# First MLP, last eight tiles: the back product as seven half-size products in place of the plain sum over sixteen steps

## The chip, the cores and the metric

The kernel runs on one core of a Trainium2 chip. The metric is the device time of one execution in microseconds (us), the median of three runs. Lower is better.

## What is computed

The reference, cut to its arithmetic. Shapes: 4 x 8 heads, 576 positions, head size 64, chunks of 64; so 2304 tokens of 512 features, 18 tiles of 128 tokens.

```python
scores = scale * np.matmul(q_c, k_c.transpose(0, 1, 2, 4, 3))     # per chunk of 64
attn = np.exp(scores - np.max(scores, axis=-1, keepdims=True))
attn = attn / (np.sum(attn, axis=-1, keepdims=True) + 1e-09)
x = np.matmul(attn, v_c)            # then heads beside each other: 2304 x 512
h = x @ w_in                        # first MLP, w_in 512 x 2048
y = (h * (1.0 / (1.0 + np.exp(-h)))) @ w_out
out = ((y @ w_a) * (y @ w_b)) @ w_out2      # second MLP, d_ff 1536
```

Weights arrive as 64-bit floats. Every product is made from operands split into a high and a low part, with three matmuls (high·high, high·low, low·high) for one.

## The kernel before, in words

The features of a token lie on the 128 partitions, so an activation tile is four column groups (`KT` = 4) of 128 x tokens. The tokens of the first MLP form five blocks: 4, 2, 4, 4 and 4 tiles (`blocks`); the block of two tiles (`SIDE`) runs beside the first one. The first MLP runs block after block, and within a block over 16 slices of d_ff (`MA` = 16). One step k is one (block, slice). `front` (`front_a`, `product`, L385) makes h for one slice, 12 matmuls of 128x512; ScalarE (ACT) applies silu twice (L413: `g` and its high part `ghi`), VectorE (DVE) takes the low part (`glo`, L411). `back` (`back_a`, L431) multiplies by w_out and adds into four PSUM banks `acc0..acc3` over the 16 slices, again 12 matmuls (4 column groups x 3). The front of step k+1 stands ahead of the back of step k in TensorE's program, so that silu and split lie beside matmuls. After the last slice the four banks are copied out and stored to DRAM (`finish_a`).

The second MLP already works on 2x2 blocks with seven products and fifteen additions (`front_product`, `back`, bank letters in `BANK`): three rounds (`PAIRS`) of 768 tokens. Its weights are needed as seven combinations, split in high and low; `comb_sums` and the splits after it make them, tiles called `ring` hold them, and DRAM buffers `wg` and `w2` keep them for later rounds.

Everything stands in a hand-written order per engine (no scheduler). In the first 16 steps (the first loop) the string `order` gives the order of the short names: `sc` = `scaled`, `mg` = `magnitude`, `bg` = `begin`, `up`/`lw` = split of a first-MLP weight, `fr` = front, `si` = its silu, `fi` = glo, `ba0`/`ba1` = halves of back, `sf`/`ss`/`sfi`/`sb` the same for the side block, S M E N T P V X L the pieces of attention for the next block (scores, maximum, exponential, normalising, transposing and copying, values and their splits). A new attention tile begins every third step.

One unit of weight conversion is a 128x512 piece of 64-bit words: a DMA into one of three raw buffers (`fetch`, SyncE's (SP's) queue), a clamp on DVE (`magnitude`, L158), two ACT operations (`scaled`, L169 and L171), and an assembly on DVE into a 32-bit tile `w` (`begin`, L181). For the second MLP `w` goes out to DRAM (`wf`). For the first MLP it is split into `wA` on ACT and DVE. Before, the first loop converts two first-MLP units a step; the 36 units of the second MLP follow, one per step, in steps 14 to 49. In the last block's steps (`in_last`) the combinations of the second MLP are made: all six of the output weight and the first of the gated ones.

Of the kernel before, what the change touches and what calls it, by code (L numbers as in the profile page):

```python
# [28 lines left out]
def chunk_attention_silu_mlp_gated_mlp(  # L29
# [50 lines left out]
    main = [b for b in range(NBLK) if b != SIDE]  # L80
    LAST = main[-1]
# [9 lines left out]
    RING = 7  # L91

# [24 lines left out]
    raws = spool.tile([P, RAWS, DM], U64, tag="raw", name="raws", bufs=1)  # L117
# [6 lines left out]
    wf = {}  # L124
    stage_1 = []
# [7 lines left out]
    def fetch(src, dest):  # L133
        raw = raws[:, turn[0] % RAWS]
        turn[0] += 1
        nc.sync.dma_start(out=raw, in_=src)
        fetched.append([dest, raw, False])
# [36 lines left out]
    def begin():  # L174
# [10 lines left out]
        if dest[0] == "f":  # L185
            wf[dest[1:]] = d = dram.tile([P, DM], F32, name=f"wf{dest[1]}{dest[2]}")
            leaving.append((d, w))
        else:
            stage_1.append((dest, w))

    def upper():
        if not stage_1:
            return
        dest, w = stage_1.pop(0)
        _, m, j = dest
        if m not in slots_a:
            slots_a[m] = slot("wA").rearrange("p (j n) -> p j n", j=4)
        hl = slots_a[m][:, 2 * j:2 * j + 2]
        nc.scalar.activation(hl[:, 0], w, AF.Copy)
        stage_2.append((dest, hl, w))  # L200
# [8 lines left out]
    def weights(src, dest):  # L209

        leave()
        fetch(src, dest)
        lower()
        scaled()
        magnitude()
        begin()
        upper()

# [11 lines left out]
    def att_tile(where, name, i=0):  # L230
        if where == "att":
# [231 lines left out]
    def comb_load(u):  # L463
        s, mat = divmod(u, 2)
        if u in (len(RING_AT) + 1, UNITS - 1):
            buf = raws[:, :2].rearrange("p a n -> p (a n)").bitcast(F32)
        else:
            buf = slot("buf", F32)
# [14 lines left out]

    def comb_split_2(s, h):
        o0, o1 = HALVES[h]
        src = bufs["o", s][:, 1 + o0:1 + o1]
        t = slot("hl").rearrange("p (o t n) -> p o t n", o=4, t=2)[:, :o1 - o0]
        nc.scalar.activation(t[:, :, 0], src, AF.Copy)
        nc.vector.tensor_tensor(
            out=t[:, :, 1], in0=src, in1=t[:, :, 0].bitcast(F32), op=ALU.subtract  # L490
        )
        w2s = w2.rearrange("p (o s) t n -> p o s t n", s=STEPS)
        nc.sync.dma_start(out=w2s[:, o0:o1, s], in_=t.bitcast(F32))
# [29 lines left out]
    kept = []  # L523
# [5 lines left out]
    def make_half():  # L529
# [3 lines left out]
        n = fed[0]  # L533
        buf = bufs[u]
# [8 lines left out]
        def lower():  # L543
# [3 lines left out]
            if n < RING:  # L547
                kept.append((wg[n], t.bitcast(F32)))
            else:
                leave()  # L550
                leaving.append((wg[n], t.bitcast(F32)))
            if h == 1 and len(RING_AT) < u + 2 < UNITS - 1:
# [11 lines left out]

    def make_now():
        make_half()
        while chores:
            chore()


# [25 lines left out]
    def refill():  # L596

        while owed[0]:
            owed[0] -= 1
            (make_half if fed[0] < 2 * UNITS else feed)()  # L600
# [6 lines left out]
    def load_pair(p, h):  # L607
        y_raw[p, h] = t = late["b"].tile([P, KT, T], F32, tag=("ca", "cb")[h], name="yr")
# [56 lines left out]
    def drain():  # L665
        leave()
        lower()
        scaled()
        magnitude()
        begin()  # L670
        upper()

# [4 lines left out]

    def prep_b():
        if done[1] < len(units_b):
            weights(*next_b())  # L680
            return True
        return False

# [10 lines left out]
    with tc.manual_schedule():  # L694
# [37 lines left out]
        def v_in(*tiles):  # L732
# [19 lines left out]
        joint = set()  # L752
# [40 lines left out]
        def plan(i, k, pos, b, o, joined, joins):  # L793
            at(k - 2, "c", lambda: load_qk(i, A))
            if joined:
                joint.add(k)
            at(k, pos, lambda: att_scores(i, (0, 1), ("at", "sB")))
# [4 lines left out]
            if joins:  # L802
                at(k + 3, "a2", lambda: att_values(i, ("at", "sB"), x_t[b], o, beside=i + 1))
# [3 lines left out]
        starts = [(2, 5, 8, 11), (18, 21, 24, 27), (33, 36, 39, 42)]  # L807
        for n, b in enumerate(main[1:]):
            at(max(starts[n][0], n * MA), "x", lambda b=b: x_t.__setitem__(b, x_tiles(width(b))))
            for t, k in enumerate(starts[n]):  # L810
                i = blocks[b][0] + t
                if n:
                    plan(i, k, "a", b, t * P, t > 0, t < 3)
                else:
                    plan_1(i, k, b, t * P)
# [3 lines left out]
        L0 = END - MA  # L819
# [95 lines left out]
        first = []  # L915

        def enter_b():
            late.pop("g")
            g_cm.__exit__(None, None, None)
            att_cm.__exit__(None, None, None)  # L920
            late["b"] = ctx.enter_context(
                tc.tile_pool(name="bpool", bufs=1, side="right", reuse_waits="tile")
            )
            for h in range(2):
                load_pair(0, h)


        def in_last(m, pos):
            if pos == "c":
                if prep_b():  # L930
                    return
                if leaving or fetched or opened or stage_1 or stage_2:
                    drain()
                if m in W2_AT:
                    comb_sums(("o", W2_AT.index(m)))
                elif m in RING_AT:
                    comb_sums(RING_AT.index(m))
                return
            if m in W2_AT:
                comb_split_2(W2_AT.index(m), int(pos == "c2"))  # L940
            if pos == "c2":
                for i in range(STEPS):
                    if W2_AT[i] == m + 2:
                        comb_load_2(i)
                for i in range(len(RING_AT)):
                    if RING_AT[i] == m + 2:
                        comb_load(i)
                if m == MA - 3:
                    comb_load(len(RING_AT))
                if m == ENTER:  # L950
                    enter_b()
            if m in RING_AT and len(ring) < RING:
                make_now()
            if m > W2_AT[-1] and kept:
                dst, src = kept.pop(0)
                nc.sync.dma_start(out=dst, in_=src)
            for f in first[:3]:
                f()
            del first[:3]

        W2_AT = [2, 3, 5, 7, 9, 11]
        RING_AT = [4, 6, 8, 10]
        ENTER = 9

        def end_last(m):
            if m == 11:
                first.extend(operands(0))

        BANKS = ("at", "sA", "sB", "mm", "acc0", "acc1", "acc2", "acc3")
        taken = [0]  # L970

        def next_bank():
            t = bank(BANKS[taken[0] % len(BANKS)], [P, T])
# [23 lines left out]
        def banks_for(o, ps):  # L997
            if o in (0, 2):
                ps[BANK[o]] = next_bank()
            return ps[BANK[o]]  # L1000

        def evacuate(o, ps, ct):
# [385 lines left out]
```

## Time and profile before

| | us |
|---|---|
| median of 3 runs (845.31 to 846.53) | 845.89 |
| the profiled execution's own time | 846.05 |
| its span, first to last instruction | 844.2 |
| TensorE (PE) busy in the span | 836.4 |
| DVE busy | 486.1 |
| ACT busy | 435.3 |
| GpSimd (POOL) busy | 54.0 |

Matmuls are pipelined, and a matmul's duration in the profile runs on into the next one; what one costs in a row is the distance between starts. The granted TensorE clock was 0.999 of full speed over the span. The execution took 1.85 us more than the span. HBM was read for 141.0 MB and written for 51.9 MB, 229 GB/s over the span.

### The profile page before, as it was taken

The page shows a single profiled execution, that of the slowest core. Times are in us where ns is not written, and L with a number is a line of the kernel's source. Part 1 is how long each engine was busy: PE and PEld are TensorE (multiplying, and loading weights), DVE is VectorE, ACT ScalarE, POOL GpSimd, SP SyncE. Part 2 cuts the span into 40 slices and gives each one's busy share as a digit, 9 for nine tenths or more (in the row PEclk, how much of TensorE's full clock was granted, in tenths as well). Part 3 has the DMA queues.
Part 4 walks back from the last instruction along what each step waited for, and adds up shares of the span by engine and source line. Part 5 has one row for each costly group of instructions (what it writes and reads, how often), then busy time and mean ns, then how long its engine had stood idle before and what let it go on. Part 6 is the DMA issues. An engine that isn't in the chain of part 4 may idle for free.

```text
span 844.2 us, 13936 instructions
## 1 busy us (share of the span) xinstructions
PE 836.4 (99%) x5442; PEld 763.5 (90%) x5442; DVE 486.1 (58%) x894; ACT 435.3 (52%) x856; POOL 54.0 (6%) x102
## 2 busy tenths in 40 slices
PE   8999999999999999999999999999999999999998
PEld 7888888888888888888889999999999999999998
DVE  5655655535444355338766997683545594454563
ACT  6956767546654566446554554462333373333252
POOL 1000000020001010023202110000000000000000
PEclk9999999999999999999999999999999999999999
DMA  8444344165555555368899788877667888666761
GB/s 300 139 161 138 131 157 147 54 231 170 174 168 175 194 185 165 121 217 319 283 381 367 305 317 321 319 279 255 259 257 274 305 304 294 244 248 245 287 236 57
DMA packets 54113, 193.85 MB, mean 230 GB/s; under 512 B 5920, under 2 KB 13728, under 8 KB 45600
## 3 DMA queue, kind: packets, MB, share of 16 engines
q1 hardware_dynamic: 46752, 169.59, 55.9%
q0 software_dynamic: 7008, 23.07, 8.3%
q8 instruction: 43, 0.70, 0.3%
q10 hardware_dynamic: 288, 0.30, 0.1%
q14 instruction: 22, 0.18, 0.1%
HBM read 141.03 MB, written 51.90 MB: 229 GB/s over the span
## 4 chain that ended last, share of the span: by engine, by line
PE 98%; DMA 1%; ACT 0%; DVE 0%; SPq 0%; issue 0%; POOL 0%
PE ps_acc L980 23%; PE ps_acc L431 21%; PE ps_mm L385 13%; PE ps_sA L385 7%; PE ps_at L980 7%; PE ps_sA L980 6%; PE ps_sB L980 5%; PE ps_mm L980 5%; PE ps_at L385 3%; PE ps_sB L431 1%; PE ps_sA L431 1%; PE ps_at L256 1%; PE ps_at L327 1%; DMA start<-kt 1%; PE ps_at L350 1%; PE ps_acc L717 0%
## 5 line engine op out<-in xcount | busy, mean ns | idle before, releaser
L980 PE MATMUL ps_acc<-xo,ring 128*128 128x384 f32 x868 | 168.1, 334 | 0.0
L431 PE MATMUL ps_acc<-ghi,wA 128*128 128x512 f32 x512 | 160.4, 394 | 0.0
L980 PEld LDWEIGHTS ps_acc<-xo,ring 128*128 128x128 f32 x868 | 152.0, 188 | 0.3 <-DVE gq L1055 0.3
L431 PEld LDWEIGHTS ps_acc<-ghi,wA 128*128 128x128 f32 x512 | 93.6, 188 | 18.9
L431 PE MATMUL ps_acc<-glo,wA 128*128 128x512 f32 x256 | 100.4, 392 | 0.0
L181 DVE SCALAR_TENSOR_TENSOR w<-raws 128x512 uint32<-128x512 uint32 x68 | 46.9, 689 | 92.4 <-ACT raws L171 92.3
L385 PE MATMUL ps_mm<-xhi,wA 128*128 128x512 f32 x320 | 86.4, 392 | 0.0
L411 DVE TENSOR_TENSOR glo<-g,ghi 128x512 fp32r<-128x512 f32 (+1 forms) x80 | 50.7, 634 | 52.1 <-ACT ghi L413 52.1
L385 PEld LDWEIGHTS ps_mm<-xhi,wA 128*128 128x128 f32 x320 | 58.7, 188 | 11.2
L413 ACT ACTIVATE g<-ps_mm 128x512 f32<-128x512 f32 x40 | 23.9, 597 | 76.9 <-PE ps_mm L385 51.8
L431 PEld LDWEIGHTS ps_acc<-glo,wA 128*128 128x128 f32 x256 | 48.1, 188 | 11.8 <-DVE glo L411 1.7
L1155 ACT ACTIVATE u<-gq 128x384 fp32r<-128x384 f32 x84 | 40.6, 516 | 30.9 <-DVE gq L1055 28.5
L1156 DVE TENSOR_TENSOR u<-gq,u 128x384 fp32r<-128x384 f32 x84 | 44.4, 552 | 15.2 <-ACT u L1155 15.0
L980 PE MATMUL ps_acc<-u,ring 128*128 128x384 f32 x272 | 52.5, 334 | 0.0
L385 PE MATMUL ps_sA<-xhi,wA 128*128 128x512 f32 x184 | 49.6, 391 | 0.0
L980 PEld LDWEIGHTS ps_acc<-u,ring 128*128 128x128 f32 x272 | 47.6, 188 | 0.0
L980 PE MATMUL ps_at<-xo,ring 128*128 128x384 f32 x231 | 47.0, 334 | 0.0
L171 ACT ACTIVATE raws<-raws 128x512 f32<-128x512 f32 x68 | 46.2, 679 | 0.0
L169 ACT ACTIVATE raws<-raws 128x512 int32<-128x512 uint8 x68 | 46.1, 678 | 0.0
L980 PE MATMUL ps_sB<-xo,ring 128*128 128x384 f32 x220 | 44.4, 334 | 0.0
L980 PE MATMUL ps_sA<-xo,ring 128*128 128x384 f32 x213 | 43.5, 335 | 0.0
L980 PE MATMUL ps_mm<-xo,ring 128*128 128x384 f32 x214 | 43.2, 334 | 0.0
(202 smaller groups left out, 1428.6 us busy)
## 6 DMA issues: line engine op xcount, KB each, us to landing
ring<-w SPq DMA_DIRECT2D x30, 1024.0 KB, 6.3
ring<-wg SPq DMA_DIRECT2D x24, 1024.0 KB, 4.9
ring<-wg SPq DMA_DIRECT2D x24, 768.0 KB, 5.7
wg<-ring SPq DMA_DIRECT2D x12, 1024.0 KB, 6.1
wf<-w SPq DMA_DIRECT2D x36, 256.0 KB, 2.2
wg<-ring SPq DMA_DIRECT2D x12, 768.0 KB, 5.5
raws<-w_in SPq DMA_DIRECT2D x16, 512.0 KB, 4.0
raws<-w_out SPq DMA_DIRECT2D x16, 512.0 KB, 4.6
```

Of the source, the lines that this page charges most:

```text
L169: nc.scalar.activation(low.bitcast(I32), top, AF.Copy, scale=2.0**-5, bias=-31 / 64)
L171: nc.scalar.activation(high, high, AF.Prelu, scale=2.0**-112, alpha=-(2.0**32))
L181: nc.vector.scalar_tensor_tensor(out=w.bitcast(U32), in0=high, scalar=3, in1=low, op0=ALU.logical_shift_left, op1=ALU.bitwise_or,)
L256: nc.tensor.matmul(soft[i][j % len(soft[i])][n, j, hp, :], lhsT=q[r, hp, n], rhs=k[r, hp, n], start=True, stop=True,)
L327: nc.tensor.transpose(ps[:, hp, :], s[:, hp, :], ident)
L385: nc.tensor.matmul(ps, lhsT=a[:, kk * P:(kk + 1) * P], rhs=b[:, kk, :], start=(j == 0 and kk == 0), stop=(j == 2 and kk == KT - 1),)
L411: nc.vector.tensor_tensor(out=glo, in0=g, in1=ghi.bitcast(F32), op=ALU.subtract)
L413: silu = [lambda out=out: nc.scalar.activation(out, ps, AF.Silu) for out in (g, ghi)]
L431: nc.tensor.matmul(acc_t[b][j], lhsT=a[:, j * P:(j + 1) * P], rhs=g, start=(m == 0 and i == 0 and (b != SIDE or j % 2 == 0)), stop=(m == M ...
L980: nc.tensor.matmul(ps, lhsT=a, rhs=b, start=first and i == 0, stop=last and i == 2, skip_group_check=True,)
L1155: nc.scalar.activation(hi, src, AF.Copy)
L1156: nc.vector.tensor_tensor(out=lo, in0=src, in1=hi.bitcast(F32), op=ALU.subtract)
```

## The change

The last two blocks (eight tiles, 1024 tokens) become a group of their own. Their 32 fronts (16 slices x 2 blocks) run one after another, without backs between them; the silu results of four fronts form one 2x2 group (two slices x two blocks), of which DVE makes the combinations. Then the back product of all 1024 tokens runs as seven products, each over eight slice pairs and two column groups, with three matmuls for each: 7 x 8 x 2 x 3 = 336 matmuls of 128x512 where 2 x 16 x 4 x 3 = 384 stood. The raw w_out goes to DRAM once more (`wo`) during conversion, and is read back, combined (`w_sum`) and split (`w_chunk`) beside the seven products (`g_work`).

Since the last blocks have no steps of their own now, other work moves:

- First loop: a new `order` with three conversions a step (`cv` = fetch and `scaled`, `af` = `begin` and `magnitude`), every third of them for the second MLP. Steps 16 to 23 take two a step.
- Attention of all eight tiles runs in steps 16 to 32, one tile every two steps (`GROUP_AT`) instead of one every three.
- The combinations of the second MLP's weights (`aux`: six of the output weight, now four gated units in place of three and a half) start at step 25 and go on beside the fronts of the group, two operations per front. Their stores go over the POOL queue (`comb_low`), and the gated units are all read back into `ring` at the end (`feed`).
- `begin_round(0)` stands behind the seventh product, and the first round's operands are made beside that product.

The core of the diff:

```diff
-    main = [b for b in range(NBLK) if b != SIDE]
+    GROUP = (NBLK - 2, NBLK - 1)
+    main = [b for b in range(NBLK) if b != SIDE and b not in GROUP]
+    SA = MA // 2
...
+            if j:
+                w2h = w.rearrange("p (h n) -> p h n", h=2)
+                leaving.append((wo[:, m % 2, :, m // 2], w2h))
             stage_1.append((dest, w))
...
+        GROUP_AT = (16, 18, 20, 22, 24, 26, 28, 30)
         order = (
-            "sc F ba1 sb fr bg sf up ba0 si N2 up lw mg fi ss T2 sc S0 V3 F X3 sfi mg lw P2 M0 E0 L3 "
-            "bg"
+            "cv ba1 sb fr af sf ba0 N2 lw up cv si fi ss T2 S0 af V3 cv X3 up sfi P2 M0 L3 E0 af lw"
         ).split()
...
+        def g_silu(n):
+            s, c = n // 4, n % 4
+            ...
+            nc.scalar.activation(g, ps, AF.Silu)
+            if c % 2 == 0:
+                ...
+                nc.scalar.activation(hi, ps, AF.Silu)
+                nc.vector.tensor_tensor(out=lo, in0=g, in1=hi.bitcast(F32), op=ALU.subtract)
+            if c == 3:
+                ...   # three DVE operations: one of 128x1024, two of 128x512
+        def g_work(o):
+            ...
+            if o == 0:
+                w_load("a21")
+                w_load("a22")
+                w_chunk(1, 0)
+                w_chunk(1, 1)
+                w_sum("s3", "a21", "a11", onto="a11")
+                w_sum("s1", "a21", "a22", ALU.add, onto="a21")
+                w_chunk(2, 0)
+                return
...
+        def fetch_next():
+            if len(fetched) + len(opened) < RAWS:
+                fetches[0] += 1
+                if done[0] < len(units_a) and fetches[0] % 3:
+                    fetch(*next_a())
+                elif done[1] < len(units_b):
+                    fetch(*next_b())
+            leave()
+        def convert():
+            fetch_next()
+            scaled()
+        def joined():
+            begin()
+            magnitude()
...
+        for n, g in enumerate([0, 2, 4, 6, 1, 3, 5, 7] + list(range(8, 4 * SA))):
+            if n > 1:
+                g_front(g)
+            ...
+            g_silu(g)
+            ...
+            if n > 3:
+                aux_op()
+                aux_op()
+            if n == 4 * SA - 12:
+                w_load("a11")
+            if n >= 4 * SA - 3:
+                w_chunk(0, n - (4 * SA - 3))
+            if n == 4 * SA - 2:
+                w_load("a12")
+        for o in range(OPS):
+            for i in range(0, SA, 2):
+                for j in range(2):
+                    g_back(o, i, j)
+                    g_back(o, i + 1, j)
+            ...
+            g_work(o)
+            for j in range(2):
+                g_done(o, j)
+            g_late(o)
```

Where instructions stand. First place: ACT in the first loop, from the values of an attention tile (`xhi`) over the next tile's exponential to the silu of the following step. L169/L171 (after: L176/L178) are the two conversion operations, L199 (L210) the split of a weight, L286 (L291) the exponential, L413 (L418) silu. Before:

```order
L362 ACTIVATE xhi<-ps_mm 128x4x64
L286 ACT_TABLE_LOAD
L286 ACTIVATE s<-s 128x512
L169 ACTIVATE raws<-raws 128x512
L171 ACTIVATE raws<-raws 128x512
L199 ACTIVATE wA<-w 128x512
L413 ACT_TABLE_LOAD
L413 ACTIVATE g<-ps_mm 128x512
L413 ACTIVATE ghi<-ps_mm 128x512
```

After:

```order
L367 ACTIVATE xhi<-ps_mm 128x4x64
L210 ACTIVATE wA<-w 128x512
L291 ACT_TABLE_LOAD
L291 ACTIVATE s<-s 128x512
L176 ACTIVATE raws<-raws 128x512
L178 ACTIVATE raws<-raws 128x512
L210 ACTIVATE wA<-w 128x512
L176 ACTIVATE raws<-raws 128x512
L178 ACTIVATE raws<-raws 128x512
L418 ACT_TABLE_LOAD
L418 ACTIVATE g<-ps_mm 128x512
L418 ACTIVATE ghi<-ps_mm 128x512
```

A second conversion now stands between the exponential and silu, and a weight split ahead of the exponential.

Second place: TensorE at the end of the first MLP (L385/L390 are fronts, L431 backs, L980/L897 the triples of the seven-product code). Before, fronts and backs alternate up to the first products of the second MLP:

```order
L385 MATMUL ps_mm<-xhi,wA 128x512 x4
L385 MATMUL ps_mm<-xlo,wA 128x512 x4
L385 MATMUL ps_mm<-xhi,wA 128x512 x4
L431 MATMUL ps_acc_3907<-ghi,wA 128x512 x2
L431 MATMUL ps_acc_3907<-glo,wA 128x512
```

After, front follows front, and the products stand behind them:

```order
L390 MATMUL ps_acc_4064<-xhi,wA 128x512 x4
L390 MATMUL ps_acc_4064<-xlo,wA 128x512 x4
L390 MATMUL ps_acc_4064<-xhi,wA 128x512 x4
L897 MATMUL ps_sA<-u,wc 128x512 x6
L897 MATMUL ps_mm<-u,wc 128x512 x6
L897 MATMUL ps_sA<-u,wc 128x512 x6
```

Third place: ACT at the turn from the fronts to the products. Before, silu and the combinations' splits (`ring`, `hl`) alternate there:

```order
L413 ACTIVATE g<-ps_mm 128x512
L413 ACTIVATE ghi<-ps_mm 128x512
L541 ACTIVATE ring<-buf 128x4x256
L413 ACTIVATE g<-ps_sA 128x512
L413 ACTIVATE ghi<-ps_sA 128x512
```

After, the last siluses, then three weight splits (`wc`; two for product 1, one for product 2), then the copy of product 0's banks into the banks in which product 1 adds:

```order
L1033 ACTIVATE gy<-ps_acc_4042 128x512
L1037 ACTIVATE u<-ps_acc_4042 128x512
L1065 ACTIVATE wc<-wr 128x4x256
L1033 ACTIVATE gy<-ps_acc_4064 128x512
L1065 ACTIVATE wc<-wr 128x4x256 x3
L906 ACTIVATE ps_acc_4148<-ps_sA 128x512
L906 ACTIVATE ps_acc_4150<-ps_mm 128x512
```

The copy that product 1 needs now stands behind a split for product 2.

## Rows read from the trace of the kernel before

**Rows 1.** The page: busy time by engine
```profile
PE 836.4 (99%) x5442; PEld 763.5 (90%) x5442; DVE 486.1 (58%) x894; ACT 435.3 (52%) x856; POOL 54.0 (6%) x102
```

**Rows 2.** The page: the chain that ended last, by engine
```profile
PE 98%; DMA 1%; ACT 0%; DVE 0%; SPq 0%; issue 0%; POOL 0%
```

**Rows 3.** Stages: length; busy of PE, PEld, DVE, ACT, POOL; clock, DMA share, GB/s
```profile
30.00:190.00 160.00, 160.00 (x1143) 136.91 (x1142) 88.70 (x178) 103.95 (x196) 9.68 (x18) 1.00 0.44 145
...
600.00:840.00 240.00, 240.00 (x1387) 240.00 (x1386) 130.47 (x233) 90.36 (x191) 0.00 (x0) 1.00 0.69 253
```

**Rows 4.** Timeline of PE, first MLP: start us, duration, instructions
```profile
346.19 1.07 PE L385 MATMUL ps_sA<-xhi,wA 128*128 128x512 f32 x4
...
348.90 0.62 PE L431 MATMUL ps_acc<-ghi,wA 128*128 128x512 f32 x2
...
351.62 1.07 PE L385 MATMUL ps_mm<-xhi,wA 128*128 128x512 f32 x4
```

**Rows 5.** The chain in order of time: start, us, what (second MLP)
```profile
553.59 12.48 PE ps_acc L980 x72
```

**Rows 6.** Timeline of PE, first loop: the fronts of four steps
```profile
96.84 1.09 PE L385 MATMUL ps_mm<-xhi,wA 128*128 128x512 f32 x4
...
105.67 1.09 PE L385 MATMUL ps_mm<-xhi,wA 128*128 128x512 f32 x4
...
115.34 1.09 PE L385 MATMUL ps_mm<-xhi,wA 128*128 128x512 f32 x4
...
123.95 1.09 PE L385 MATMUL ps_mm<-xhi,wA 128*128 128x512 f32 x4
```

**Rows 7.** Timeline of ACT, then DVE: the conversion and its clamp
```profile
39.75 0.70 ACT L169 ACTIVATE raws<-raws 128x512 int32<-128x512 uint8 x1
40.48 0.68 ACT L171 ACTIVATE raws<-raws 128x512 f32<-128x512 f32 x1
...
40.02 0.42 DVE L158 TENSOR_SCALAR raws<-raws 128x512 f32<-128x512 f32 x1
...
104.81 0.69 DVE L181 SCALAR_TENSOR_TENSOR w<-raws 128x512 uint32<-128x512 uint32 x1 [0.81 <-ACT raws L171]
105.42 0.69 DVE L206 TENSOR_TENSOR wA<-w,wA 128x512 fp32r<-128x512 f32 x1
```

**Rows 8.** Timeline of ACT, DVE, then PE: the step behind an exponential
```profile
114.51 0.63 ACT L286 ACTIVATE s<-s 128x512 f32<-128x512 f32 x1
...
118.34 1.28 ACT L413 ACT_TABLE_LOAD   x1 [1.56 <-PE ps_mm L385]
119.63 0.60 ACT L413 ACTIVATE g<-ps_mm 128x512 f32<-128x512 f32 x1
...
120.75 0.69 DVE L411 TENSOR_TENSOR glo<-g,ghi 128x512 fp32r<-128x512 f32 x1 [2.83 <-ACT ghi L413]
...
121.49 0.50 PE L431 MATMUL ps_acc<-glo,wA 128*128 128x512 f32 x1
```

**Rows 9.** Landing of raw-weight DMAs: 0 to 30, 60 to 110, w_o 100 to 200
```profile
DMA to landing us min/median/max: 3.5/6.6/6.9
...
DMA to landing us min/median/max: 3.5/4.4/4.8
...
DMA to landing us min/median/max: 4.1/4.2/4.2
```

**Rows 10.** Timeline of SP's queue: a store, and the fetch behind it
```profile
189.95 0.33 SPq L143 DMA_DIRECT2D wf<-w  x1
190.37 0.38 SPq L136 DMA_DIRECT2D raws<-w_o  x1
```

**Rows 11.** The page: DMA issues, KB each, median us to landing
```profile
ring<-w SPq DMA_DIRECT2D x30, 1024.0 KB, 6.3
ring<-wg SPq DMA_DIRECT2D x24, 1024.0 KB, 4.9
```

**Rows 12.** Groups by form: busy us, mean ns, idle before (DVE, 128x1024)
```profile
L544 DVE TENSOR_TENSOR ring<-buf,ring 128x1024 fp32r<-128x1024 f32 x10 | 12.2, 1219 | 0.5 <-ACT ring L541 0.3
```

**Rows 13.** A stretch with combinations (columns as rows 3), then landing of `buf`
```profile
440.00:450.00 10.00, 10.00 (x51) 8.97 (x50) 5.71 (x8) 5.78 (x10) 0.00 (x0) 1.00 1.02 428
...
DMA to landing us min/median/max: 3.0/5.7/9.7
```

More of the change, by code (lines that the diff above doesn't have):

```diff
@@ L133, in fetch @@
     def fetch(src, dest):
-        raw = raws[:, turn[0] % RAWS]
+        raw = raws[0][:, turn[0] % RAWS]
         turn[0] += 1
@@ L230, in att_tile @@
     def att_tile(where, name, i=0):
+        if where == "att" and name in "qk" and "g" in late:
+            return late["g"].tile([P, DM], F32, tag="qk", name=name, bufs=2)
         if where == "att":
@@ L546, in lower @@
             )
[L547 to L552, printed above, removed]
+            leave()
+            leaving.append((wg[n], t.bitcast(F32)))
+            if h == 1 and EARLY + 1 < u + 2 < UNITS - 1:
                 comb_load(u + 2)
@@ L910, in chunk_attention_silu_mlp_gated_mlp, with next_bank @@
         shared.clear()
[L915 to L969, printed above, removed]
+        BANKS = ("sA", "mm", "acc0", "acc1", "at", "sB", "acc2", "acc3")
         taken = [0]
-        def next_bank():
-            t = bank(BANKS[taken[0] % len(BANKS)], [P, T])
+        def next_bank(n=T):
+            t = bank(BANKS[taken[0] % len(BANKS)], [P, n])
             taken[0] += 1
@@ new lines, in g_open, with g_take @@
+        def g_open():
+            pass
+        def g_take(s, y):
+            if s == 0:
+                g_units[s, y] = [
+                    gpool.tile([P, DM], F32R, tag=tg, name="u") for tg in ("ghi", "glo")
+                ]
+                return
+            if y and s > 2:
+                t = late["gun"].tile([P, 2, DM], F32R, tag=f"u{s}", name="u")
+                g_units[s, y] = t[:, 0], t[:, 1]
+            elif s < 3 or s > 5:
+                if (s, y) not in g_units:
+                    t = slot("u").rearrange("p (u t n) -> p u t n", u=2, t=2)
+                    pair = ((s, 0), (s, 1)) if s < 3 else ((6, 0), (7, 0))
+                    for i, key in enumerate(pair):
+                        g_units[key] = t[:, i, 0], t[:, i, 1]
+            elif (s, y) not in g_units:
+                t = spool.tile([P, 6, DM], F32R, tag="raw", name="u", bufs=1)
+                for i in range(3):
+                    g_units[3 + i, 0] = t[:, 2 * i], t[:, 2 * i + 1]
@@ new lines, in w_sum, with g_back @@
+        def w_sum(dst, a, b, op=ALU.subtract, onto=None):
+            if onto:
+                wr[dst] = wr[onto]
+            elif dst not in wr:
+                wr[dst] = slot("wr", F32).rearrange("p (s n) -> p s n", s=SA)
+            a, b = wr[a], wr[b]
+            for h in range(2):
+                n = slice(4 * h, 4 * h + 4)
+                nc.vector.tensor_tensor(out=wr[dst][:, n], in0=a[:, n], in1=b[:, n], op=op)
+        xg = [{}, {}]
+        def g_back(o, i, j):
+            ps = banks_for(o, xg[j], DM) if i == 0 else xg[j][BANK[o]]
+            t = w_ring[o, i // 4]
+            w = [t[:, i % 4, h, j * P:(j + 1) * P] for h in range(2)]
+            triple(ps, w, g_units[i, o % 2], o in (0, 2) and i == 0, i == SA - 1)
@@ new lines, in g_done @@
+        def g_done(o, j):
+            if o == 1 and not g_out:
+                g_out.append(slot("y", F32).rearrange("p (c n) -> p c n", c=4))
+                for b in GROUP:
+                    y_dram[b] = [dram.tile([P, 2, DM], F32, name=f"y{b}{h}") for h in range(2)]
+            t = g_out[0] if g_out else None
+            ct = [None] * 4 if t is None else [t[:, j], t[:, j], t[:, j], t[:, 2 + j]]
+            evacuate(o, xg[j], ct, DM)
+            c = {1: 0, 4: 3, 5: 1, 6: 2}.get(o)
+            if c is not None:
+                nc.sync.dma_start(out=y_dram[GROUP[c % 2]][c // 2][:, j], in_=ct[c])
```

333 lines of the change are left out of this document (220 added, 113 removed).

## The prediction, made before the changed kernel was run

> **What bounds the kernel now.** The page first: TensorE is busy for 836.4 of 844.2 us [rows 1], and the chain that ended last is 98% PE [rows 2]. The stages say the same: from 30 to 190 us and from 600 to 840 us PE has no idle slice, at a granted clock of 1.00 [rows 3], the upper of its two levels (2.4 GHz). So a matmul taken out of the stream is worth its full spacing, as long as every operand still comes in time. Then the timeline of PE for that spacing: twelve matmuls of a front go from 346.19 to 348.90, twelve of a back from 348.90 to 351.62 [rows 4], so 2.72/12 = 0.2267 us for one of 128x512. Then the first loop's timelines, because the change makes it convert half as much again per step: how long a conversion's chain is, and how long its load takes to land. The execution's own time is 846.05, 1.85 over its span and 0.16 over the median of 845.89; I sum against 846.05 and give the result as a median.
>
> **Matmuls.** Removed are 2 x 16 x 4 x 3 = 384 back matmuls, added 7 x 8 x 2 x 3 = 336; the fronts stay. 48 fewer x 0.2267 = **-10.9 us**. Could the new ones be dearer, since three matmuls share a bank and the next three may go to another? The second MLP's code does just this: 72 matmuls of 128x384 in 12.48 us [rows 5], 0.173 each, three quarters of 0.2267 (0.170) within 2%. By the 0.003 between them for 336 matmuls it would be 1.0 us less gain; I leave that in the range.
>
> **First loop, engines.** One more conversion per step is two ACT operations of 0.69, a DVE clamp of 0.42 and an assembly of 0.69 [rows 7], 1.38 on ACT and 1.11 on DVE. Some 18 steps lie in the 160 us of [rows 3], so ACT goes from 104.0 to 129 us and DVE from 88.7 to 109: room in the mean. In sequence: steps are 8.83 (transposes), 9.67 (values, scores, exponential) and 8.61 us (silu behind a table load) from front to front [rows 6]. A clamp and its L171 form a ping-pong, since L171 waits for the clamp (40.02 + 0.42, L171 at 40.48) and the clamp of the next unit stands behind the assembly, which waits for L171 [rows 7]. One round is 0.04 + 0.68 + 0.04 + 0.60 + 0.42 = 1.78 us; the round with silu and `glo` in it comes to some 3.4. Three rounds are 2 x 1.78 + 3.4 = 7.0, in the step with the table load 1.28 more [rows 8], 8.2. Both fit, the last by 0.4. There the conversion that now stands ahead of silu makes `glo` about 0.15 late per tile; before, `glo` ended at 121.44 and its matmul started at 121.49 [rows 8], so it was just on the edge too, 0.1 to 0.25 late per tile.
>
> **First loop, landings.** Here I expect the loss. The buffer of a unit is free after the assembly of the unit three earlier, and the clamp of the new one is due two rounds later; with L from that assembly to the landed data, a late clamp delays the conversions that ACT has queued ahead of silu, then `g`, `ghi` and `glo`, and PE waits in the back. Followed through three steps, `glo` behind a table load is 0.15 + max(0, 2L - 8.82) late: L = 4.7 gives 0.7 per tile, 5.0 gives 1.3, 5.3 gives 1.9. What is L? The critical fetch now stands right behind a store on SP's queue, and such a pair is issued 0.42 apart (189.95, 190.37) [rows 10], plus 0.05 for the assembly's end. Landing: 4.2 in the median for the `w_o` loads between 100 and 200 us that stand behind a store, 4.4 (at most 4.8) for 60 to 110 us, 6.6 in the first 30 us, where loads crowd [rows 9]. So L is 4.7 by the rows nearest in code, 5.3 by the largest of a quiet stretch, 7.1 by the crowded one. Traffic in the stage rises from 145 GB/s [rows 3] to some 2.6 MB per 9.1 us step, about 286 GB/s, between the quiet stretch and the crowd; I take 5.0. The first tile has spare buffers and costs 0.15; three tiles cost 1.3 each: 4.1. About 1 us of such lateness is in the time before. Net **+3**, from 0 (L up to 4.4) to 5 (L 5.3), and open above that.
> The Trainium skill ("DMA: Bandwidth & Descriptors", section "Anatomy of one DMA — SWDGE (gpsimd) path") fits one DMA as 2.0 us and its bytes over 436 GB/s, for transfers that GpSimd issues; for these 512 KB an estimate by it is 3.2 us. By that L would be 3.7 and this term nothing, the time 836.5 instead of 839.3. The rows disagree: no raw weight landed in under 3.5 us and the medians are 4.2 to 6.6 [rows 9], so the measurement decides.
>
> **Up to step 32.** Where the first loop ends, the side block's last work and the accumulators' copies stand behind conversions: 0.3 (0 to 1). In steps 16 to 31 attention has one tile per two steps, 12.4 us of PE work; I count 10.9 us of ACT and 8.7 of DVE in them while conversions last: 0.2 (0 to 1.6).
>
> **The fronts of the group.** 32 fronts of 2.72 us take 87 us. There are eight banks, so PE can run seven fronts (19 us) ahead of silu; that covers a late silu. What stands beside them: the combinations, whose DMAs move about 2.36 MB per two fronts (5.44 us), 434 GB/s, where 428 GB/s was the most seen, with PE still unbroken, and a `buf` landed in 5.7 us in the median, 9.7 at most [rows 13]. At 360 GB/s the lag over the 17 fronts that carry them is 10 us, under the 19 that the banks cover: **0**. With every load at 9.7 the lag is some 23 us, 4 us more than the cover; that is a rival.
>
> **The turn from product 0 to product 1.** Product 1 adds into banks into which ACT copies product 0's (L906), and the copy stands behind a split for product 2 (L1065), which needs a DVE sum of two loaded pieces (`a21`, `a22`). These loads can start only as the fronts end, since they reuse the silus' room; 1 MB each, 4.9 us the first [rows 11], the next a transfer time later, so `a22` is there some 7.9 us after the fronts' end. The sum takes 1.2 [rows 12], split and copy some 2: the copy is done at 11.2, product 0 at 48 x 0.2267 = 10.9. Stall 0.3; with loads landing in 6.3, as the other 1 MB loads did [rows 11], 1.9. I take **+0.8**. Later products have at most 10.9 us of ACT or DVE work in as many of PE, the structure with which the second MLP keeps PE unbroken [rows 3]: 0.
>
> **Sum.** 846.05 - 10.9 + 3.0 + 0.3 + 0.2 + 0.8 = 839.45; as a median **839.3 us**, a gain of 0.8%.
>
> **The rivals.**
> *Full gain.* If L stays at 4.4 or below, the loads are hidden as now, and with a small turn it is about 836.5. For it: the `w_o` loads at 4.2 [rows 9]. Against it: those stood in half the traffic. The Trainium skill's fit ("DMA: Bandwidth & Descriptors", the section named above) leads to this rival too.
> *Slower.* The landing rises to that of the crowded first 30 us, 6.6, because three loads of 512 KB a step and the new store share the queues: L = 7.1, three tiles at 0.15 + 14.2 - 8.82 = 5.5 each, and as the clamps fall behind, the other steps wait too: 16.6 for the tiles alone, time at least 852. It eats the whole gain when three tiles cost 11 + 1 (what is there now), 4.0 each, L = 6.35, a landing of 5.9. For it: [rows 9] shows 6.6 with 128x512 loads from the same inputs. Against it: 286 GB/s is well below the 428 that the chip moved elsewhere [rows 13].
> *Half of it.* Landing between 5.3 and 5.8 in the first loop, or the combinations' loads at 9.7, so that the group's fronts wait 4 us: 843 to 846.
> *The change doesn't save matmuls on the path.* The order of the changed kernel has 48 fewer; excluded.
>
> **How the numbers follow.** Forecast 839.3 with its own range of 837.5 to 842.5: 0.55. Full gain: 0.17. Half of it: 0.16. Slower: 0.12. A measurement here can tell about 0.2%, 1.7 us: faster is under 844.2, same 844.2 to 847.6. Forecast and full gain lie in faster, of half of it a third or so; the rest of it is same, save a little of its top: 0.77, 0.11, and 0.12 for slower. The range leaves out the slower rival, the top of half of it and a little of full gain: 835.5 to 846.5.
>
> **What would show it.** The matmul count falls by 48, and the seven products take 0.227 us per matmul. In the first loop, raw loads land in about 4.5 us, and fronts are spaced wider by about 1.3 us in the step that carries the silu table load, the wait being for `glo`; full gain shows no wider step, the slower rival landings over 6 us and all steps wide. No idle PE between the group's fronts; idle there, with silu waiting for a `buf`, is the third rival. One PE wait of under 2 us at product 1's first matmul, for the copy on ACT. I am wrong in the working if the loss sits anywhere else: in steps 16 to 32, at the entry of the products, or in the second MLP, whose rows I took as unchanged.

## The result, and the profile after

The changed kernel takes 853.77 us in the median (853.40 to 859.48) against 846.06 before: ratio 1.0108, 95% interval 1.0065 to 1.0151, slower by about 1%. The profiled execution is the 859.48; the three others lie at 853.4 to 853.9. So its trace shows more loss than the median has, and sizes are taken from medians of runs where there are any.

The page of the changed kernel, engines and the chain that ended last:

```profile
PE 832.2 (97%) x5394; PEld 757.8 (88%) x5394; DVE 550.0 (64%) x972; ACT 468.4 (55%) x900; POOL 65.4 (8%) x118
...
PE 80%; DMA 9%; ACT 5%; DVE 3%; issue 2%; SPq 0%; POOL 0%; DVEq 0%; ACTq 0%
```

The 48 matmuls are gone (5394 for 5442), but PE's busy time fell by 4.2 us only, and the chain, 98% PE in [rows 2], now goes through DMA and ACT. The span grew by 13.5 us. PE idles 25.5 us (857.7 - 832.2) where it idled 7.8 (844.2 - 836.4 [rows 1]), 17.7 more; and its busy time is 6.7 us above 836.4 - 10.9 = 825.5, for the most part because some of it ran at a lower clock. 17.7 + 6.7 - 10.9 = 13.5.

Where? Three stretches of the changed kernel (length, busy time of PE, PEld, DVE, ACT, POOL, clock, DMA share, GB/s), then two of PE's waits from 30 to 190 us and both from 190 to 240 (in all, times, longest):

```profile
30.00:190.00 160.00, 146.98 (x1027) 124.50 (x1026) 97.79 (x199) 117.24 (x215) 5.89 (x11) 0.97 0.70 227
190.00:240.00 50.00, 46.71 (x408) 37.48 (x407) 32.17 (x69) 38.87 (x68) 7.51 (x15) 0.97 0.91 312
240.00:600.00 360.00, 360.00 (x2047) 320.67 (x2046) 263.62 (x415) 194.41 (x331) 47.25 (x76) 1.00 0.65 238
```

```profile
PE ps_at L261 <- ACT ghi L418: 6.0, 3, 3.2
PE ps_acc L436 <- ACT ghi L418: 4.9, 2, 3.3
...
PE ps_at L261 <- ACT pt L336: 2.2, 1, 2.2
PE ps_acc L436 <- DVE y L455: 1.1, 1, 1.1
```

All of the loss lies ahead of 240 us. From there to 600 us, with the group's fronts, the seven products and the turn between them, PE has no idle slice. In the first loop PE waits for silu's `ghi`. Front by front, it ends 19.6 us later than before (a front at 192.80 for one at 173.20). The first and the last of these fronts, before and then after:

```profile
29.53 1.17 PE L385 MATMUL ps_mm<-xhi,wA 128*128 128x512 f32 x4
...
173.20 1.07 PE L385 MATMUL ps_mm<-xhi,wA 128*128 128x512 f32 x4
```

```profile
29.31 1.18 PE L390 MATMUL ps_mm<-xhi,wA 128*128 128x512 f32 x4
...
192.80 1.07 PE L390 MATMUL ps_mm<-xhi,wA 128*128 128x512 f32 x4
```

That is 163.5 us for 143.7, 19.8 more: 13.0 of them idle (160.00 - 146.98), 6.8 busy. Three steps hold most of it, 14.0, 11.6 and 14.4 us wide where 9.2, 9.7 and 8.6 stood. The three steps behind 192.80 are 4.4 us longer than the same steps of e5 below, in which PE waits for 0.4.

And the products themselves, on PE's timeline: the first of their matmuls, then the first of the second MLP behind them.

```profile
384.23 1.52 PE L897 MATMUL ps_sA<-u,wc 128*128 128x512 f32 x6
...
460.41 1.23 PE L897 MATMUL ps_acc<-xo,ring 128*128 128x384 f32 x6
```

76.18 us for 336 matmuls, as worked out from [rows 4].

Why is silu late? Follow one load of `w_out` through the changed kernel, in a step in which silu loads its table. First SP's queue, then ACT, then DVE, then PE:

```profile
91.97 0.41 SPq L143 DMA_DIRECT2D raws<-w_out  x1
...
105.43 0.38 SPq L150 DMA_DIRECT2D wo<-w  x1
105.91 0.41 SPq L143 DMA_DIRECT2D raws<-w_out  x1
```

```profile
100.43 0.70 ACT L176 ACTIVATE raws<-raws 128x512 int32<-128x512 uint8 x1 [3.27 <-DMA raws<-w_out]
101.03 0.65 ACT L178 ACTIVATE raws<-raws 128x512 f32<-128x512 f32 x1
101.70 1.28 ACT L418 ACT_TABLE_LOAD   x1
102.99 0.60 ACT L418 ACTIVATE g<-ps_mm 128x512 f32<-128x512 f32 x1
103.48 0.59 ACT L418 ACTIVATE ghi<-ps_mm 128x512 fp32r<-128x512 f32 x1
```

```profile
104.11 0.69 DVE L416 TENSOR_TENSOR glo<-g,ghi 128x512 fp32r<-128x512 f32 x1 [2.71 <-ACT ghi L418]
104.72 0.68 DVE L188 SCALAR_TENSOR_TENSOR w<-raws 128x512 uint32<-128x512 uint32 x1
```

```profile
104.13 1.22 PE L436 MATMUL ps_acc<-ghi,wA 128*128 128x512 f32 x2 [3.28 <-ACT ghi L418]
```

The load is issued at 91.97 and its conversion starts at 100.43. Silu stands behind that conversion on ACT, `glo` behind silu, the assembly (L188) behind `glo` on DVE. Only when the assembly has ended, at 105.40, do the store and then the next `w_out` load go out, at 105.91, because with three units a step and three buffers that load has this very buffer. That is a closed circle, once per step: 13.94 us here, of which 8.41 from issue to the landed data and 5.5 of work and queue. PE's step is about 9. The landings of raw weights from 60 to 190 us, and what ACT waits for `w_out` from 30 to 190:

```profile
DMA to landing us min/median/max: 3.7/5.0/8.4
...
ACT raws L176 <- DMA raws<-w_out: 24.9, 12, 4.8
```

The clock falls behind the longest of these waits. PE at 60.80, behind 3.18 us of idle, and the stretch a little later:

```profile
60.80 0.27 PE L261 MATMUL ps_at<-k,q 64*64 64x64 f32 x1 [3.18 <-ACT ghi L418]
```

```profile
62.00:66.00 4.00, 4.00 (x18) 3.66 (x17) 3.06 (x8) 3.97 (x6) 0.40 (x1) 0.57 0.77 225
...
104.00:111.00 7.00, 6.87 (x24) 5.96 (x25) 4.87 (x10) 4.71 (x10) 0.00 (x0) 0.56 0.64 178
```

For 4 us the granted clock is 0.57, most of it at the lower level (1.2 GHz), after which it is back at 1.00. Behind the 3.28 us of idle that end at 104.13 it is 0.56 for 7 us.

### The profile page after: what moved, and what is told of

Same layout as the page of the kernel before. It is cut to its first block, busy times and chain, and to the rows that moved or that the text cites. A ratio compares the mean times of both kernels' runs of the same rounds, so it can differ in the third digit from the quotient of the medians.

```text
span 857.7 us, 14083 instructions
## 1 busy us (share of the span) xinstructions
PE 832.2 (97%) x5394; PEld 757.8 (88%) x5394; DVE 550.0 (64%) x972; ACT 468.4 (55%) x900; POOL 65.4 (8%) x118
## 4 chain that ended last, share of the span: by engine, by line
PE 80%; DMA 9%; ACT 5%; DVE 3%; issue 2%; SPq 0%; POOL 0%; DVEq 0%; ACTq 0%
PE ps_acc L897 26%; PE ps_sA L897 8%; PE ps_mm L897 8%; PE ps_sB L897 7%; PE ps_at L897 7%; PE ps_acc L436 6%; DMA raws<-w_out 5%; PE ps_acc L390 5%; PE ps_mm L390 5%; PE ps_sA L390 3%; PE ps_at L390 2%; DMA raws<-w_o 2%; PE ps_sB L390 1%; DVE w L188 1%; ACT raws L178 1%
## 5 line engine op out<-in xcount | busy, mean ns | idle before, releaser
L897 PE MATMUL ps_acc<-xo,ring 128*128 128x384 f32 x902 | 171.9, 334 | 0.0
L897 PEld LDWEIGHTS ps_acc<-xo,ring 128*128 128x128 f32 x902 | 157.7, 188 | 0.4 <-DVE gq L972 0.3
L436 PE MATMUL ps_acc<-ghi,wA 128*128 128x512 f32 x256 | 84.2, 411 | 6.1 <-ACT ghi L418 4.9
L176 ACT ACTIVATE raws<-raws 128x512 int32<-128x512 uint8 x68 | 46.8, 689 | 34.0 <-DMA raws<-w_out 24.9
L390 PE MATMUL ps_mm<-xhi,wA 128*128 128x512 f32 x224 | 61.6, 397 | 0.2
L188 DVE SCALAR_TENSOR_TENSOR w<-raws 128x512 uint32<-128x512 uint32 x68 | 46.8, 689 | 23.0 <-ACT raws L178 21.2
L897 PE MATMUL ps_acc<-u,ring 128*128 128x384 f32 x322 | 61.3, 334 | 0.0
L436 PEld LDWEIGHTS ps_acc<-ghi,wA 128*128 128x128 f32 x256 | 46.8, 194 | 16.4 <-ACT ghi L418 6.2
L897 PEld LDWEIGHTS ps_acc<-u,ring 128*128 128x128 f32 x322 | 56.3, 188 | 0.0
L178 ACT ACTIVATE raws<-raws 128x512 f32<-128x512 f32 x68 | 45.5, 669 | 11.9 <-DVE raws L165 11.7
L436 PE MATMUL ps_acc<-glo,wA 128*128 128x512 f32 x128 | 51.6, 403 | 0.0
L390 PEld LDWEIGHTS ps_mm<-xhi,wA 128*128 128x128 f32 x224 | 40.9, 190 | 8.0 <-PE ps_sB L436 0.6
L165 DVE TENSOR_SCALAR raws<-raws 128x512 f32<-128x512 f32 x68 | 28.8, 423 | 28.4 <-DMA raws<-w_out 21.7
L416 DVE TENSOR_TENSOR glo<-g,ghi 128x512 fp32r<-128x512 f32 (+1 forms) x48 | 28.7, 598 | 26.2 <-ACT ghi L418 26.1
L897 PE MATMUL ps_sA<-xo,ring 128*128 128x384 f32 x220 | 44.4, 334 | 0.0
L906 ACT ACTIVATE gq<-ps_acc 128x384 f32<-128x384 f32 x31 | 15.3, 492 | 52.8 <-PE ps_acc L897 49.7
L897 PE MATMUL ps_mm<-xo,ring 128*128 128x384 f32 x214 | 43.2, 334 | 0.0
L897 PE MATMUL ps_sB<-xo,ring 128*128 128x384 f32 x208 | 42.3, 335 | 0.0
L897 PE MATMUL ps_at<-xo,ring 128*128 128x384 f32 x202 | 41.0, 334 | 0.0
L897 PEld LDWEIGHTS ps_sA<-xo,ring 128*128 128x128 f32 x220 | 38.7, 188 | 0.0
```

The source lines that it names most:

```text
L165: nc.vector.tensor_scalar(out=high, in0=high, scalar1=LARGEST, scalar2=-LARGEST, op0=ALU.min, op1=ALU.max)
L176: nc.scalar.activation(low.bitcast(I32), top, AF.Copy, scale=2.0**-5, bias=-31 / 64)
L178: nc.scalar.activation(high, high, AF.Prelu, scale=2.0**-112, alpha=-(2.0**32))
L188: nc.vector.scalar_tensor_tensor(out=w.bitcast(U32), in0=high, scalar=3, in1=low, op0=ALU.logical_shift_left, op1=ALU.bitwise_or,)
L390: nc.tensor.matmul(ps, lhsT=a[:, kk * P:(kk + 1) * P], rhs=b[:, kk, :], start=(j == 0 and kk == 0), stop=(j == 2 and kk == KT - 1),)
L416: nc.vector.tensor_tensor(out=glo, in0=g, in1=ghi.bitcast(F32), op=ALU.subtract)
```

## The experiments

Theory A: the landing of raw weights, in that circle, costs the first loop. Rivals: B, three conversions a step are too many for ACT and DVE wherever the loads are; C, the attention loads on GpSimd's queue are what delays the raw loads; D, another part of the change loses time too. Each run's "before" is the kernel before on the same chip, 845.5 to 845.6, some 0.5 us under the 846.06 above; differences to the changed kernel are those of the medians as they stand.

**e1: two conversions a step.** The first loop's order, fetch and clamp of the kernel before; the second MLP's units all wait until the first MLP's are through.

```diff
-            "cv ba1 sb fr af sf ba0 N2 lw up cv si fi ss T2 S0 af V3 cv X3 up sfi P2 M0 L3 E0 af lw"
+            "sc F ba1 sb fr bg sf up ba0 si N2 up lw mg fi ss T2 sc S0 V3 F X3 sfi mg lw P2 M0 E0 L3 "
+            "bg"
...
-                if done[0] < len(units_a) and fetches[0] % 3:
+                if done[0] < len(units_a):
```

> The first loop goes back to two conversions a step, in the order of the kernel before; all 36 units of the second MLP are converted from step 14 on, two a step, to the first fronts of the group. Theory A (a raw weight's landing sets the first loop: its load is issued only when the same unit of the step before is assembled): the loop is as before, no wait of PE from 30 to 170 us, and the product's gain stands: 836 to 840. Rival B (three conversions are too many for ACT and DVE in their order, wherever the loads are): the same here for the first loop. Rival D (steps 16 to 31 can't take two conversions a step beside attention): waits of PE between 170 and 270 us grow to 5 us or more, 842 to 848.

Measured: 842.94, ratio 0.9969 (0.9957 to 0.9982). The first loop has no wait of PE up to 120 us and under 1 us to 150; but steps 16 to 31, now with two conversions beside attention throughout, wait 2.9 us for `pt` in three places, and the copies of the accumulators for 1.6. So the third conversion in the first loop is what cost most, and D holds in part. It doesn't tell A from B.

**e2: two more raw buffers** in steps 1 to 11 (one free 8 KB slot of the large pool), filled by two loads ahead.

```diff
-        raw = raws[0][:, turn[0] % RAWS]
-        turn[0] += 1
+        raw = free.pop(0)
...
+                t = slot("raws2", F32).rearrange("p (a n) -> p a n", a=2)
+                free[:0] = [t[:, i].bitcast(U64) for i in range(2)]
+                fetch_next()
+                fetch_next()
```

> Two more raw buffers in steps 1 to 11, filled by two loads ahead; orders unchanged. Theory A: a load has some 5 us more time, ACT no longer waits for data in these steps, some 12 us of the first loop's loss go: 840 to 844. Rival B (engines' order): the loads are earlier, PE waits as long as in the changed kernel: 851 to 855.

Measured: 839.42, ratio 0.9922 (0.9906 to 0.9939), 14.3 us under the changed kernel. A, and a little over what it expected; B is out: ACT and DVE do the same operations in the same order. The first loop from 30 to 190 us, then the landings from 60 to 190:

```profile
30.00:190.00 160.00, 159.11 (x1133) 134.72 (x1131) 109.01 (x224) 132.78 (x238) 9.67 (x18) 1.00 0.80 268
...
DMA to landing us min/median/max: 3.7/4.9/8.0
```

The loads land as late as in the changed kernel, and more bytes move per second (268 GB/s for 227). So neither the landing by itself nor the traffic costs the time, but a landing that the next load has to wait for.

**e3: silu ahead of the second conversion.**

```diff
-            "cv ba1 sb fr af sf ba0 N2 lw up cv si fi ss T2 S0 af V3 cv X3 up sfi P2 M0 L3 E0 af lw"
+            "cv ba1 sb fr af sf ba0 N2 lw up si fi cv ss T2 S0 af V3 cv X3 up sfi P2 M0 L3 E0 af lw"
```

> In the first loop silu and its low part stand ahead of the second conversion of a step, not behind it; loads and buffers unchanged. Theory A: the late load (its conversion stood ahead of silu) no longer delays silu, and the circle from load to assembly loses silu's 2 us: 841 to 847, PE's waits for ghi in the first loop fall under half. Rival B: the conversions are pushed back instead and weights come late: 850 to 856.

Measured: 844.86, ratio 0.9995 (0.9977 to 1.0012). The waits for `ghi` are down to one of 1.2 us, as A wants, but five new ones for the side block's `glo` come in, 2.0 us in all: the conversion now stands between the two siluses.

**e4: half of each raw load** in the first 16 steps, but for the first ones, which stay whole.

```diff
-        nc.sync.dma_start(out=raw, in_=src)
+        n = DM if done[0] < 4 or not late.get("half") else DM // 2
+        nc.sync.dma_start(out=raw[:, :n], in_=src[:, :n])
```

> In the first 16 steps every raw load carries only half its columns (256 KB of 512); the other half of a weight is whatever lay in the buffer, all operations stay. Theory A: loads land in 3.0 to 3.5 us, ACT waits little for data, 839 to 844. Rival B: no change, 851 to 855. Rival C (the attention loads on GpSimd's queue, which come together with the worst landings, are what costs): the landings of 6 to 8 us remain in every third step, 847 to 851.

Measured: 840.47, ratio 0.9938 (0.9923 to 0.9952). The landings from 60 to 190 us (the 7.7 is a full load behind the loop):

```profile
DMA to landing us min/median/max: 2.5/3.2/7.7
```

Same operations, same buffers, 13.3 us less than the changed kernel with half the bytes in each load and so shorter landings. That is A once more.

**e5: e2, and `pt` ahead of the second conversion** in steps 16 to 31. The reason is in e2's trace: SP's queue, ACT, then PE at step 17.

```profile
181.79 0.33 SPq L146 DMA_DIRECT2D raws<-w_o  x1
...
189.90 0.68 ACT L179 ACTIVATE raws<-raws 128x512 int32<-128x512 uint8 x1 [3.93 <-DMA raws<-w_o]
190.46 0.65 ACT L181 ACTIVATE raws<-raws 128x512 f32<-128x512 f32 x1
191.02 0.58 ACT L341 ACTIVATE pt<-ps_at 128x512 f32<-128x512 f32 x1
...
191.65 0.27 PE L266 MATMUL ps_at<-k,q 64*64 64x64 f32 x1 [1.99 <-ACT pt L341]
```

This load goes out right behind the stores of the block's result and the loads of q, k and v, and takes 8 us; ACT stands at its conversion for 3.9, and `pt`, whose transposes were ready long before, is queued behind it.

```diff
-            "fr a a2 cv c fi af d au ba cv b e af"
+            "fr a a2 cv c fi af d au ba b cv e af"
```

> The version with two more raw buffers, and in steps 16 to 31 the transposes of attention and their copy on ACT (pt) stand ahead of a step's second conversion instead of behind it. Theory A for what is left there (one load of 8.0 us at step 17 holds ACT, pt is queued behind it, PE waits 2.0 us and runs on at the lower clock): that wait and its 1.5 to 2 us of slow matmuls go, 835 to 838. Rival B (the step is too full for ACT, whatever the order): another wait takes its place, 838.5 to 840.

Measured: 837.48, ratio 0.9897 (0.9881 to 0.9914), 1.9 us under e2; the longest of its executions took 837.73, the shortest of e2 838.89. The stretch in which e2 had 48.35 of 50 us busy at a clock of 0.97:

```profile
190.00:240.00 50.00, 50.00 (x462) 41.02 (x462) 33.51 (x74) 41.43 (x70) 8.26 (x15) 1.00 0.81 277
```

**e6: stores of the first loop over GpSimd's queue.**

```diff
-            nc.sync.dma_start(out=dst, in_=src)
+            (nc.sync if late.get("sp") else nc.gpsimd).dma_start(out=dst, in_=src)
```

> The changed kernel with three raw buffers; the stores of converted weights in the first 16 steps go over GpSimd's queue, not SP's, so that a load isn't issued 0.46 us behind a store. Theory A with the circle of load, landing and assembly closed in every step: about 0.46 us per step for 14 steps, 845 to 849. Rival (only the steps with a late landing pay): under 2 us less, 852 to 854.

Measured: 848.98, ratio 1.0042 (1.0023 to 1.0061), 4.8 us under the changed kernel. It fits what the store ahead of the load would cost in a circle closed in every step, but doesn't show it cleanly: new waits come with it, 3.3 us for a load of `k` that now stands behind a store on GpSimd's queue, and 2.6 for the side block's `glo`.

**e7: half of the attention loads** in steps 4 to 15.

```diff
-            eng.dma_start(out=a, in_=src[i])
+            eng.dma_start(out=a[:, :n], in_=src[i][:, :n])
+            if n < DM:
+                nc.gpsimd.memset(a[:, n:], 0.0)
```

> The changed kernel with three raw buffers; from step 4 to 15 the attention loads q, k and v carry half their columns, the other half is zero (written by GpSimd); all operations stay. Theory C (the loss is the attention loads' traffic beside the raw load): the landings of 6 to 9 us fall under 5.5, 846 to 849. Theory A without C (the circle alone, at 4.5 to 5 us of landing): 851 to 854.

Measured: 852.77, ratio 1.0083 (1.0068 to 1.0098). The worst landings from 60 to 190 us are shorter:

```profile
DMA to landing us min/median/max: 3.5/4.8/6.1
```

It brings 1.0 us: taking the top off these landings hardly helps. C isn't out altogether. The first late load of the loop goes out at 51.1 us, behind loads of q and k that are still whole; it lands in 6.3 us (6.6 in the changed kernel), and PE's step there is 13.7 us wide for 14.0. So e7 doesn't show what that one landing costs.

**e8: the assembly ahead of silu.** One word moves in the first loop's order; `af` is the assembly with the clamp behind it, so both move.

```diff
-            "cv ba1 sb fr af sf ba0 N2 lw up cv si fi ss T2 S0 af V3 cv X3 up sfi P2 M0 L3 E0 af lw"
+            "cv ba1 sb fr af sf ba0 N2 lw up cv af si fi ss T2 S0 V3 cv X3 up sfi P2 M0 L3 E0 af lw"
```

> The changed kernel with three raw buffers; in the first loop the assembly that follows a step's second conversion (and the clamp behind it) stands ahead of silu and its low part on DVE, not behind them. The load that reuses this buffer can then be issued about 2 us earlier (3.3 where silu loads its table), while silu still stands behind the conversion on ACT. Theory A, closed circle (load, landing, conversion, silu, low part, assembly, next load, once per step): without silu in it the circle is 0.46 + 4.5 + 1.3 + 0.7, about 7 us, shorter than a step; only single late landings still cost, 842 to 847. Rival (silu's wait for the landing is what costs, and the circle is not closed): 850 to 854.

Measured: 840.62, ratio 0.9943 (0.9928 to 0.9959), 13.2 us under the changed kernel, and better than expected. SP's queue in a step with a table load, and DVE there:

```profile
94.08 0.41 SPq L143 DMA_DIRECT2D raws<-w_out  x1
...
102.74 0.38 SPq L150 DMA_DIRECT2D wo<-w  x1
103.22 0.41 SPq L143 DMA_DIRECT2D raws<-w_out  x1
```

```profile
92.88 0.69 DVE L188 SCALAR_TENSOR_TENSOR w<-raws 128x512 uint32<-128x512 uint32 x1
...
95.28 1.03 DVE L416 TENSOR_TENSOR glo<-g,ghi 128x512 fp32r<-128x512 f32 x2 [1.37 <-ACT ghi L418]
```

The assembly ends at 93.57, ahead of `glo`, and the load goes out at 94.08, while silu is still loading its table. Silu still stands behind the conversion on ACT; what is gone is silu's place in the circle. One new wait comes with it, 1.5 us of PE for `glo` at 42.45.

**e9: e5, and silu ahead of the second conversion.** The edit of e3 upon that of e5.

> The version with two more raw buffers and pt ahead of the second conversion, now also with silu ahead of the second conversion in the first loop. What the trace of it shows left over in the first loop is 0.36 us per step with a table load, four of them. If the conversion ahead of silu is that, 836 to 837.3 (1 us less than without); if the conversions are pushed into the weights' way instead, 837.5 to 840.

Measured: 841.13, ratio 0.9946 (0.9933 to 0.9958), 3.6 us over e5 and above both ranges. PE waits in four steps for the side block's low part, and the steps of the first loop are 0.13 to 0.5 us wider each from 51 us on:

```profile
PE ps_sA L441 <- DVE glo L421: 1.4, 4, 0.3
```

With the loads out of the way a conversion between the two siluses only costs. Where it stood, ahead of both, was the better place.

**e10: e3, e6 and `pt` ahead of the conversion**, three buffers.

> No more memory: three raw buffers, silu ahead of the second conversion, the stores of the first loop on GpSimd's queue, pt ahead of the second conversion in steps 16 to 31. Theory A: the circle is 0.05 + 4.5 + 1.3 + 0.7 and silu waits for no load, 837.5 to 841. If stores on GpSimd's queue or late landings still hold weights up: 841 to 846.

Measured: 849.66, ratio 1.0044 (1.0031 to 1.0056). It is worse than e3 alone, and above both ranges. One of PE's waits, and GpSimd's queue:

```profile
PE ps_at L261 <- DMA k<-kt: 3.1, 3, 1.2
```

```profile
78.86 0.72 POOL L150 DMA_DIRECT2D wo<-w  x1 [5.67 <-DVE w L188]
79.57 0.56 POOL L246 DMA_DIRECT2D q<-qt  x1
80.12 0.66 POOL L246 DMA_DIRECT2D k<-kt  x1
```

The store waits on GpSimd for its assembly, and the loads of q and k stand behind it; PE waits for k in the next step. The side block's `glo` waits add 3.3 us.

**e11: e8 and `pt` ahead of the conversion**, three buffers: two orders changed, no memory.

> Three raw buffers; the assembly ahead of silu in the first loop, and pt ahead of the second conversion in steps 16 to 31: orders alone, no memory. The two causes lie in different stages (first loop; step 17's wait of 1.8 us and the wide step behind it), so they should add: 840.6 less 2 to 3, 837.5 to 839. If the wait only moves to another place: 839.5 to 841.

Measured: 838.69, ratio 0.9920 (0.9907 to 0.9932). The two causes add, 13.2 and 1.9.

**e12: e5 and e8 together.**

> Two more raw buffers, pt ahead of the second conversion, and the assembly ahead of silu. With five buffers the circle is no longer closed within a step, so the assembly's place should not matter: 837 to 838, the same as without it. If the 0.36 us left over in each step with a table load come from the assembly or clamp behind silu, 836 to 837.

Measured: 838.18, ratio 0.9915 (0.9902 to 0.9929), no better than e5 (0.9897, intervals overlap). With five buffers the circle isn't closed within a step, and moving the assembly brings nothing. It isn't without effect: the steps with a table load are 0.1 us narrower than in e5, and one early step is 1.8 us wider, with the wait that e8 has too:

```profile
PE ps_acc L441 <- DVE glo L421: 1.5, 1, 1.5
```

## Why the prediction was wrong, point by point

The time, 853.8, is outside the range, and on the side of the rival that had 0.12.

*The matmuls* were right to 0.02 us: 76.18 for 76.2. With e5 the kernel gains 8.1 us of the 10.9.

*The engines in the first loop* were near. With e2's buffers three steps with a table load are 8.97 us wide (8.61 in [rows 6]) and one 8.70, the others as before: 0.36 us three times and 0.1 once, where I had 0.15 per tile. Silu ahead of the conversion (e9) didn't take it away, the assembly ahead of silu (e12) took 0.1 of each, so its cause is open.

*The landings* are the step that failed. I wrote that the clamp of a new load is due two rounds after the assembly that frees its buffer, and priced what is late once per tile, as 0.15 + max(0, 2L - 8.82), with +3 us for the stage. Both the form and the size were wrong.

The form: I treated the assembly's time as given and asked how late the data would come. But the assembly stands behind `glo`, `glo` behind silu and silu behind the conversion of the load itself, so a late load delays its own successor, in every step and not per tile. The sum that I didn't make is short: 0.5 to the issue, 4.5 landing, 1.3 conversion, 1.1 silu, 0.6 `glo`, 0.7 assembly, 8.7 us, and 10.0 with the table load: 27.4 for three steps that take 27.1 [rows 6]. At the landing that I took the circle had no slack left, and by this sum each 0.5 us of landing more is 0.5 us per step. Ten of e7's loads of `w_out`, from 42.1 us to 139.3, follow each other by 9.7 us, where PE's step before is 9.0; ten of e2, where no circle closes, by 8.8. The sum isn't exact: these ten of e7 landed in 4.5 us in the mean, for which it gives 9.1, so 0.6 stays open. e8 shows the same cause with one word moved. And the wait was for `ghi`, not for `glo` as I had it, and not in the steps with a table load alone.

The size: the term is 14.3 us by e2, 13.2 by e8, for 3. The landing itself, 5.0 in the median, was near the 4.5 of my L = 5.0, with five of the twelve for which ACT waited at 5.7 to 8.4. Shortening some of the late ones brought 1.0 us in e7; with the circle opened, landings of 3.4 to 7.4 us (4.9 in the median) do little harm in e8. The 4.2 that I set beside them was the median of two loads, both behind 170 us.

*The slower rival* gave at least 852 and named the stage, but for a landing of 6.6 in general. Its number came out at a median of 5.0, by the circle and not by the landing that it named; and its deciding landing of 5.9 was wrong with the same formula.

*The clock* had no term at all. I charged an idle PE its idle time only. In the profiled execution the first loop holds 6.8 us more busy time of PE for the same matmuls, and these delay it as idle time does. The two stretches at 0.57 and 0.56 make some 4.8 of them, an estimate from their lengths and what their clock lacks to 1.00; the rest isn't settled. In the first 30 us the clock was low too (0.89), but there PE is busy for less time than before (24.4 us for 25.8), and the first front isn't later (29.31 for 29.53).

*Steps 16 to 31* had 0.2 us from sums of ACT's and DVE's work. They cost 1.9 by e5 against e2: not work, but one load of 8 us with `pt` queued behind its conversion. In the profiled execution the step with that wait is 3.7 us wider than in e5, 2.2 of them idle and the rest behind it, where the clock fell.

*The fronts of the group* at 0 were right: no idle from 240 to 600 us, so the rival of the combinations' loads is out. *The turn* at 0.8 was of the right size for e1 (0.7) and e5 (0.4), by the wait that I named, for the copy on ACT; the changed kernel has no wait there. The two loads went out 0.9 to 2.5 us ahead of the fronts' end in these three, and not at it, as I had them. (The 836.5 beside the 839.3 in the prediction is 836.3 as a median.)

What is left of the gain in e5, 2.8 us under 10.9: 1.2 for the steps with a table load, and by its waits 0.4 each for the accumulators' copies and the turn and 0.3 for a load of `ring` behind the products; the rest isn't settled.

## What to carry to other kernels

Before adding work to a loop with few load buffers, close the circle: from the issue of a load over its landing and everything that stands ahead of its release on in-order engines to the next issue into the same buffer, and compare that with the step. If it is close, move the release ahead of whatever doesn't need it (one word here was worth 13 us, with one new wait of 1.5), or add a buffer; moving the consumer instead, or its stores to another in-order queue, brought new waits. And sums of busy time say nothing about an operation queued behind one that waits for a transfer.

## What the runs showed of the hardware that I had not expected

An idle PE costs more than its idle time: 3.18 us without a matmul were followed by a stretch of 4 us at a granted clock of 0.57, 3.28 us by one of 7 us at 0.56.

Raw loads of half the size landed in 3.2 us in the median (2.5 at least) where whole ones took 5.0 (3.7), so 256 KB more cost 1.2 to 1.8 us. The Trainium skill ("DMA: Bandwidth & Descriptors", section "Anatomy of one DMA — SWDGE (gpsimd) path") gives 0.6 us for these bytes, an estimate by its fit for transfers that GpSimd issues. The least landings lie nearer to it than the medians, which other transfers share; these runs don't part the two.
